# Attention beside a state-space convolution: x relaid out by VectorE instead of GpSimd, and zero matmuls sized to what a group lacks

## The chip, the cores and the metric

The kernel runs on one core of a Trainium2 chip. The metric is the device time of one execution in microseconds; a time is the median of several runs. The engines that matter are TensorE (PE in the profile; its weight loads are PEld), ScalarE (ACT), VectorE (DVE), GpSimd (POOL) and SyncE (SP, which here issues nearly all DMAs). Each engine works through its own list of instructions in order; semaphores make one engine wait for another.

## The reference

Two branches work on the same x (2048 rows of 512, bf16) and are mixed by a gate. In short:

```python
g = sigmoid((x * gate_w).sum(-1, keepdims=True))
# A: attention, 32 heads of 16, no mask
q, k, v = split(x @ wqkv)
a = softmax(q @ k.T * 16 ** -0.5) @ v     # per head, 2048 x 2048 scores
a = a @ wo
# B: a state-space layer: a causal convolution along the rows, 512 channels, 128 states each
P = exp(dt * A * l)                       # l = 0..2047, complex
K = einsum(C, P, dt * B).real             # 512 x 2048
b = causal_conv(x, K) + x * Dskip
return g * a + (1 - g) * b
```

## The kernel before

**The two branches.** Attention is cut into 32 blocks b (a quarter of the queries, a pair of key/value column groups, one of two head parities) and each block into 16 steps kt of 128 keys. One step has four score tiles of 128 x 512, one per row group of the array. ScalarE takes three score tiles at a time: a *group* g is one `ex(g)`, an exponential of 128x1536 from a PSUM tile SC (three banks) to the ring ET; there are 683 groups. `qk(g)` makes the three score tiles of a group with three matmuls of 32 rows each, and two SC tiles alternate, so the scores of group g + 1 can be made while ScalarE works on group g, and those of g + 2 only when g is done. `pv(q)` multiplies four tiles of ET by V with four matmuls of 32 columns each, which add up in the bank OA over the 16 steps of a block. At a block's end `norm_a` transposes OA to SBUF (VectorE, L704), `norm_b` divides by the sums, and OA is free for the next block.

The state-space branch is done in chunks of 64 rows. VectorE builds the powers of the transition (params, base, table: L718 and others). Then, for each of four quarters qr of the channels: the x rows of the chunks are multiplied into states on TensorE (`sstage`, evicted from PSUM bank MB at L1006), a scan over 32 chunks runs on VectorE (L1026 to L1042), and the output is formed on TensorE (`ystage`, evicted at L1114). This work needs x in another layout: with 64 positions of a chunk on partitions and chunk and channel along the free axis. `rows` loads it from a DRAM copy of x with two DMAs (L1129, issued by SP), into XS for the states and into XR for the output. In this layout an element's channel is the inner index and the chunk the outer one (32 x 64), while the matmuls want 64 channels by 32 chunks. GpSimd turns it round: two multiplications by a half mask hm per quarter, from XS to XZ (L1141), and one copy per quarter from XR to X2 (L1151). XZ is the moving operand of the state matmuls, X2 that of the local part of the output.

The projections, the gate, the convolution's kernel and the final projection use the bank MB as well, one user at a time (a lock in the scheduler), and VectorE evicts it.

**What sets the order.** The order on every engine is laid down when the program is made. `record` walks through the groups. For each it emits `ex(g)` and `qk(g + 1)`, then calls `sch.fill(t, .5, zeros, quiet())`, where t is the planned end of the exponential on ScalarE. The scheduler holds threads (Python generators: `pvs`, `norms`, `qms`, `projs`, `ystage`, `scan`, `ublks`, `ulocals` and so on). Each yields an engine, a planned cost and a priority ahead of a few instructions, and may ask for marks of others (AFTER) or for MB (LOCK). `fill` issues the thread that can start earliest, as long as it can start before t, and for TensorE work of lower rank ends before t + 0.5. Planned costs stand in the code; a DMA is planned with its issue cost, a latency, and LATE (2.0) more before its reader may start. AFTER marks order the plan alone; on the chip only data dependences wait.

**Zero matmuls.** `wm` is a tile of zeros. `zeros()` multiplies it (128 x 128 by 128 x 512) into OA, so it adds nothing to an open block. It is issued in two places: in `fill`, ahead of a background TensorE piece of lower rank, and at a group's end while TensorE's planned time is before t. It needs an open block (`sch.now`, set by `sch.open` after each `pv` and set to None after the last step of a block). At most two are issued per group. `p.act` adds up the activity of what was issued: a matmul's columns times the share of the array that it fills (128 for one score or one PV matmul, 512 for a zero matmul). After each group `lack[0]` gains FILL (1300) minus `p.act`, held between 0 and 512; `zeros()` issues when `lack[0]` is at least 256. Besides, the groups run in cycles of 17. In 12 of them state and output matmuls ("low" pieces) may be issued; in the other 5, the quiet ones, low pieces wait and zero matmuls are issued whatever `lack` says.

All matmuls are recorded in the helper at L562, so the profile's groups are told apart by their tiles.

Of the kernel before, what the change touches and what calls it, by code (L numbers as in the profile page):

```python
# [20 lines left out]
CB = D // NBLK  # L21
HALF_PI = math.pi / 2
NDSEM = 56
FILL = 1300
NS = 15
SGH = 144
NSG = 2
LATE = 2.0
CYCLE, LOWS = 17, 12
VW = 152  # L30


# [205 lines left out]
class Sched:  # L238


    def __init__(self, prog):
        self.p = prog
        self.thr = []
        self.flag = set()
        self.lock = {}
        self.now = None
        self.n = 0

    def add(self, gen, prio):
# [12 lines left out]
        else:  # L262
            self.flag.add(name)

    def open(self, b):
        if self.p.cap is not None:
            self.p.cap.append(lambda: self.open(b))
        else:
            self.now = b

    def unlock(self, name):
        if self.p.cap is not None:
# [4 lines left out]
    def pull(self, t):  # L277
        t.conds, t.seg = [], None
        y = t.nxt
        if y is None:  # L280
            y = next(t.gen, None)
        while y is not None and y[0] in ("AFTER", "LOCK"):
            t.conds.append(y)
            y = next(t.gen, None)
        if y is None:
            assert not t.conds
            return
        t.eng, t.cost = y[0], y[1]
        t.up = y[2] if len(y) > 2 else t.prio
        t.low = len(y) > 3  # L290
        assert self.p.cap is None
        self.p.cap = []
        t.nxt = next(t.gen, None)
        t.seg, self.p.cap = self.p.cap, None
        if t.nxt is None:
            t.gen = iter(())
# [29 lines left out]
        if t.seg is None:  # L326
            self.thr.remove(t)

    def fill(self, until, slack, zeros, quiet=False):
        while True:  # L330
            best = None
            for t in self.thr:
                if t.low and quiet:
                    continue
                e = self.est(t)
                if e is None or e > until or t.eng == "PE" and t.up > 0 and e + t.cost > until + slack:
                    continue
                now = self.p.tm[t.eng]
                k = (max(e, now + .3) if e > now + .02 else now, t.up, t.n)
                if best is None or k < best[0]:  # L340
                    best = (k, t)
            if best is None:
                break
            if best[1].eng == "PE" and best[1].up > 0 and zeros():
                continue
            self.issue(best[1])
        while self.p.tm["PE"] < until and zeros():
            pass

    def force(self, name):  # L350
# [12 lines left out]
class Thread:  # L363

    def __init__(self, gen, prio, n):
        self.gen, self.prio, self.n = gen, prio, n
        self.nxt = None
        self.conds, self.seg, self.eng, self.cost, self.up, self.low = [], None, None, 0, prio, False


def declare(nc, es):
# [76 lines left out]
    for k in range(4):  # L448
        sb(f"X2{k}", 32 * 64)
        sb(f"XZ{k}", 2 * 32 * 64)  # L450
        sb(f"XS{k}", 32 * 64)
        sb(f"XR{k}", 32 * 64)

    sb("Py", 3 * 2 * 16 * T)
# [92 lines left out]
def record(nc, p, B, ins):  # L547
# [533 lines left out]
    def ystage():  # L1081
        yield ("AFTER", "gp")

        def unit(u):
            blk, hf = divmod(u, 2)
            qr, bl = divmod(blk, 4)
            sg, r = SG[qr % NSG], u % 3
            yield ("AFTER", f"scan{qr}")
            yield ("AFTER", f"ul{qr}")
            yield ("AFTER", f"yl{u}")  # L1090
            yield ("LOCK", "MB")
            ky = [(MB, 0, ('y', u))]
            for k in range(8):
                if k % 4 == 0:
                    yield ("PE", .28, 2, True)
                kk = 8 * hf + k
                mm(lambda k=k: MB(32 * k, [[1, 32]]), lambda k=k: Tt(r * 1024 + 128 * k, [[1, 128]]),
                   lambda kk=kk: X2[qr](32 * (16 * bl + kk), [[1, 32]]),
                   [(X2[qr], 0)] + [(Tt, (r, par, k // 4), u) for par in range(2)] + [(Tt, "z")], ky, k == 0, False, c=.1 if k % 4 == 0 else .06, a=32)
            for k in range(8):  # L1100
                if k % 2 == 0:
                    yield ("PE", .48, 2, True)
                kk = 8 * hf + k
                for ri in range(2):
                    for par in range(2):
                        i = 2 * k + par
                        mm(lambda k=k, par=par: MB(32 * k, [[1, 32]], 64 * par, 64),
                           lambda ri=ri, i=i: Py(r * YN + ri * 16 * T + i * T, [[1, T]]),
                           lambda ri=ri, kk=kk, par=par: sg(ri * SGH + CB * bl + 2 * kk + par, [[2 * SGH, 32]]),
                           [(sg, (bl, b_), (qr, 'G')) for b_ in range(4)] + [(sg, "z"), (Py, r, u)], ky, False, ri == 1,  # L1110
                           pos=(0, 64 * par), c=.1 if k % 2 == ri + par == 0 else .056, a=16)
            sch.mark(f"yu{u}")
            yield ("DVE", .4, -1)
            op("DVE", lambda v: v.tensor_tensor(Yl(16 * blk + 8 * hf, [[256, 32], [1, 8]]), MB(0, [[1, 32], [32, 8]]),  # L1114
                                                B["g1"](0, [[1, 32], [0, 8]]), ALU.mult), ky + key("g1"), [(Yl, u)], c=.38)
            sch.unlock("MB")
            if u % 8 == 7:
                sch.mark(f"yq{qr}")

        for u in range(2 * NBLK):  # L1120
            yield from unit(u)

    hm = B["hm"]
    poolq = [(hm, "q")]

    def rows(b, qr):
        for par in range(2):
            yield ("SP", 1.9)
            dma("SP", lambda e, par=par: e.dma_start(b(0, [[64, 32], [1, 64]], 64 * par, 64),  # L1129
                                                     B["xrd"].dram(64 * qr + 256 * par, [[32 * D, 64], [D, 32], [1, 64]])),  # L1130
                [(B["xrd"], 0)], [(b, par)], c=1.9, lat=5)

    def ublocks(qr):
        XS = B[f"XS{qr}"]
        yield ("AFTER", f"yu{8 * qr - 12}" if qr >= 2 else f"S{4 * qr - 2}" if qr else "base3")
        yield from rows(XS, qr)
        if qr:
            yield ("AFTER", f"S{4 * qr - 1}")
        for h in range(2):
            yield ("POOL", 3.5)  # L1140
            op("POOL", lambda g, h=h: g.tensor_scalar(XZ[qr](32 * h, [[64, 64], [1, 32]]), XS(0, [[1, 64], [64, 32]]), hm(h, [[1, 1]]), None, ALU.mult),  # L1141
               [(XS, 0), (XS, 1), (hm, 0)], [(XZ[qr], h)] + poolq, c=3.5)
        sch.mark(f"ub{qr}")

    def ulocal(qr):
        XR = B[f"XR{qr}"]
        yield ("AFTER", f"S{4 * qr + 3}")
        yield ("AFTER", "K15")
        yield from rows(XR, qr)
        yield ("POOL", 3.5)  # L1150
        op("POOL", lambda g: g.tensor_copy(X2[qr](0, [[32, 64], [1, 32]]), XR(0, [[1, 64], [64, 32]])),  # L1151
           [(XR, 0), (XR, 1)], [(X2[qr], 0)] + poolq, c=3.5)
        sch.mark(f"ul{qr}")

    def ublks():
# [105 lines left out]
    def pvs():  # L1261
        for q in range(NQ - 1):
            b, kt = divmod(q, 16)
            if kt == 0 and b >= 1:
                yield ("AFTER", f"n{b - 1}")
            if b < 8 and b % 2 == 0 and kt % 4 == 0:
                yield ("AFTER", f"V{b // 2}.{kt // 4}")
            yield ("PE", QUAD)
            pv(q)
            sch.mark(f"pv{q}")  # L1270
            sch.open(b if kt < 15 else None)

    def norms():
        for b in range(31):
            yield ("AFTER", f"pv{16 * b + 15}")
            yield ("DVE", .75, -2)
            norm_a(b)
            sch.mark(f"n{b}")
            yield ("DVE", .65, 1)
            norm_b(b)  # L1280
            if b % 2 == 1:
                yield ("DVE", .7, 1)
                norm_c(b)
# [62 lines left out]
    def quiet():  # L1346
        return p.q % CYCLE >= LOWS

    def zeros():
        b = sch.now  # L1350
        if lack[0] < 256 and not quiet() or lack[1] == 2 or b is None:
            return False
        mm(lambda: OA(0, [[1, 512]]), lambda: wm(0, [[1, 128]]), lambda: wm(0, [[1, 512]]), [(wm, 0)], [(OA, 0, b)], False, False)
        lack[0] -= 512
        lack[1] += 1
        p.act -= 512
        return True

    for g in range(NG):
# [8 lines left out]
            need(g + 1)  # L1368
            qk(g + 1)
        t = p.tm["ACT"]  # L1370
        sch.fill(t, .5, zeros, quiet())
        lack[0] = max(min(lack[0] + FILL - p.act, 512), 0)
        p.act = lack[1] = 0
    while sch.thr:
        p.q += 1
        sch.fill(1e9, 1e9, lambda: False)
        assert p.q < NG + 50, [(t.conds, t.eng, t.prio) for t in sch.thr]

    p.q += 1
# [46 lines left out]
```

## Time and profile before

| | |
|---|---|
| median of three runs | 1041.11 us (1034.61, 1041.11, 1050.18) |
| the profiled execution | 1036.27 us, its span 1034.5 us |
| granted TensorE clock, mean over the span | 0.81 |
| instructions in the trace | 17282 |
| HBM read, written | 30.02 MB, 25.17 MB |
| share of 16 DMA engines, queue q1 | 29.8% |
| x rows XS, XR: DMAs of 256 KB | 8 and 8; 5.1 and 5.3 us from issue to landing (median) |

The page gives, after the busy time of each engine, the span in 40 slices of 25.9 us. A digit is the busy share in tenths; PEclk is the share of TensorE's full clock that was granted. Of a group of instructions it gives line, engine and operation, the tiles written and read, shape and number, then busy time and mean duration (ns), then the engine's idle time just before them and what ended most of it. In a timeline each row has start, duration, engine, line and operation; the idle time before it and its releaser stand in square brackets. A table of stretches gives, for each, its length, the busy time and number of instructions per engine (PE, PEld, DVE, ACT, POOL), the granted clock, the DMA share and GB/s.

The mean duration of a matmul holds its passage through the array; matmuls behind each other start closer than that.

### The profile page before, as it was taken

Reading aid. Unit: us, or ns where it says so; the run is one execution under the profiler, and the core shown is the slowest. Engines: PE = TensorE matmul, PEld = TensorE weight load, DVE = VectorE, ACT = ScalarE, POOL = GpSimd, SP = SyncE. Lnnn points to the kernel's source line nnn. Section 1 sums busy time; section 2 is a strip of 40 time slices with the busy share of each in tenths; the row PEclk is TensorE's granted clock in tenths of the full one; section 3 lists DMA queues with packets and bytes.
Section 4 is the critical chain, followed back from the end, with each engine's and each line's share of the span. In section 5 each row is a group of like instructions: output and inputs, shape, how many; then the busy total and the mean of one; then the engine's idle time right before and its main releaser. Section 6 shows DMA issues by size and latency. Waiting matters only on the chain.

```text
span 1034.5 us, 17282 instructions
## 1 busy us (share of the span) xinstructions
PE 868.8 (84%) x7323; PEld 280.1 (27%) x7323; DVE 663.5 (64%) x1329; ACT 936.9 (91%) x693; POOL 89.8 (9%) x28
## 2 busy tenths in 40 slices
PE   7888858898968799878858988499889998987896
PEld 3233222222322222112312223132233333332211
DVE  5899989977796888898992259951299411131202
ACT  6999959999969999988959999499999999899995
POOL 4000230000050000120320010500100000000000
PEclk9999969877858977766958689666898799699866
DMA  8200100028655556261413464034212221010000
GB/s 178 82 2 1 22 1 1 1 93 199 152 90 151 143 143 152 115 128 52 98 51 67 67 123 98 26 78 59 44 52 78 77 78 52 11 37 16 1 1 21
DMA packets 171469, 73.35 MB, mean 71 GB/s; under 512 B 150272, under 2 KB 159104, under 8 KB 169344
## 3 DMA queue, kind: packets, MB, share of 16 engines
q1 hardware_dynamic: 169088, 71.07, 29.8%
q10 hardware_dynamic: 2304, 1.18, 0.6%
q8 instruction: 57, 0.93, 0.4%
q14 instruction: 20, 0.16, 0.1%
HBM read 30.02 MB, written 25.17 MB: 53 GB/s over the span
## 4 chain that ended last, share of the span: by engine, by line
ACT 52%; PE 28%; DVE 17%; DMA 1%; issue 1%; ACTq 0%; DVEq 0%
ACT ET L690 52%; PE OA L562 14%; PE SC L562 9%; PE MB L562 5%; DVE G L1039 3%; DVE s L1032 2%; DVE s L1035 2%; DVE SG L1042 2%; DVE s L1029 2%; DVE tt L718 1%; DVE ft L718 1%; DVE Qm L666 1%; DVE SG L1006 1%; DMA Wq<-in_A_wqkv_dram 1%; DVE ON L709 1%
## 5 line engine op out<-in xcount | busy, mean ns | idle before, releaser
L690 ACT ACTIVATE ET<-SC 128x1536 bf16<-128x1536 f32 (+1 forms) x683 | 929.8, 1609 | 81.2 <-PE SC L562 79.6
L562 PE MATMUL SC<-Qm,KT 32*128 32x512 bf16 x2048 | 310.8, 449 | 89.1 <-ACT ET L690 81.4
L562 PE MATMUL OA<-ET,VE 128*32 128x512 bf16 x2048 | 239.3, 458 | 30.5 <-DVE OT L704 29.6
L562 PE MATMUL OA<-wm 128*128 128x512 bf16 x587 | 233.2, 454 | 1.2 <-DVE wm L615 1.2
L562 PEld LDWEIGHTS SC<-Qm,KT 32*128 32x128 bf16 x2048 | 68.0, 93 | 288.0 <-ACT ET L690 219.0
L1006 DVE TENSOR_TENSOR SG<-MB,sgn 128x496 bf16<-128x496 f32 x64 | 42.9, 670 | 94.7 <-PE MB L562 94.6
L562 PEld LDWEIGHTS OA<-ET,VE 128*32 128x32 bf16 x2048 | 54.2, 96 | 179.0 <-issue 140.9
L1141 POOL TENSOR_SCALAR XZ<-XS,hm 128x2048 bf16<-128x2048 bf16 x8 | 59.8, 7481 | 282.9 <-DMA XS<-gm_xrd 170.1
L562 PEld LDWEIGHTS OA<-wm 128*128 128x128 bf16 x587 | 43.4, 100 | 120.0 <-issue 118.8
L718 DVE TENSOR_TENSOR tt<-B,D 128x1024 bf16<-128x1024 bf16 x96 | 67.1, 734 | 0.5
L704 DVE STREAM_TRANSPOSE OT<-OA 128x512 f32<-128x512 f32 x32 | 22.8, 713 | 60.8 <-PE OA L562 60.7
L1039 DVE TENSOR_TENSOR G<-s,s 128x256 f32<-128x256 f32 x120 | 59.2, 493 | 3.4
L1114 DVE TENSOR_TENSOR Yl<-MB,g 128x256 bf16<-128x256 f32 x32 | 13.4, 419 | 73.3 <-PE MB L562 73.1
L1032 DVE TENSOR_TENSOR s<-G,MU 128x256 f32<-128x256 f32 x120 | 58.8, 490 | 0.0
L1035 DVE TENSOR_TENSOR s<-s,SG 128x256 f32<-128x256 f32 x120 | 55.4, 461 | 0.0
L562 PE MATMUL MB<-XZ,Qt 128*128 128x64 bf16 x512 | 40.9, 216 | 12.9 <-DVE SG L1006 12.2
L1029 DVE TENSOR_TENSOR s<-G,MU 128x256 f32<-128x256 f32 x120 | 50.1, 418 | 0.1
L562 PE MATMUL MB<-SG,Py 128*64 128x32 bf16 x1024 | 47.3, 233 | 2.2 <-DVE SG L1042 2.2
L562 PEld LDWEIGHTS MB<-XZ,Qt 128*128 128x128 bf16 x512 | 29.7, 110 | 44.8 <-issue 27.3
L666 DVE TENSOR_SCALAR Qm<-Q,msk 128x512 bf16<-128x512 bf16 x31 | 17.4, 562 | 35.0 <-PE SC L562 35.0
L1042 DVE CAST SG<-G 128x256 bf16<-128x256 f32 x120 | 37.6, 313 | 3.5
L718 DVE TENSOR_TENSOR ft<-FP,L 128x1024 f32<-128x1024 f32 (+1 forms) x32 | 39.1, 1244 | 0.3
(128 smaller groups left out, 513.5 us busy)
## 6 DMA issues: line engine op xcount, KB each, us to landing
gm_ptd<-PT SPq DMA_DIRECT2D x16, 1024.0 KB, 6.1
Py<-gm_ptd SPq DMA_DIRECT2D x32, 512.0 KB, 4.1
gm_kpd<-Kst SPq DMA_DIRECT2D x16, 256.0 KB, 2.5
Tt<-gm_kpd SPq DMA_DIRECT2D x128, 32.0 KB, 3.3
gm_xrd<-in_A_x_dram SPq DMA_DIRECT2D x1, 2048.0 KB, 12.0
XS<-gm_xrd SPq DMA_DIRECT2D x8, 256.0 KB, 5.1
XR<-gm_xrd SPq DMA_DIRECT2D x8, 256.0 KB, 5.3
out_dram<-fo SPq DMA_DIRECT2D x28, 64.0 KB, 2.1
```

Source lines behind the costliest of these rows:

```text
L562: op("PE", lambda t: t.matmul(out(), lhsT(), rhs(), start=start, stop=stop, skip_group_check=True, **kw), R, W, c=c, lat=.15, a=a)
L666: op("DVE", lambda v: v.tensor_scalar(Qm(512 * (b % 2), [[1, 512]]), B[f"Q{qc}"](512 * pi, [[1, 512]]), msk(w, [[1, 1]]), None, ALU.mult), ...
L690: op("ACT", lambda a: a.activation(ET(512 * e, [[1, 512 * n]]), sc(0, [[1, 512 * n]]), AF.Exp, scale=DH ** -0.5), [(sc, i, g) for i in ran ...
L704: op("DVE", lambda v: v.transpose(OT(0, [[1, 512]]), OA(0, [[1, 512]])), [(OA, 0, b)], [(OT, 0, b)], c=.72)
L718: op(eng, lambda v: v.tensor_tensor(o(), a(), b_(), f), R, W, c=c)
L1006: op("DVE", lambda v, bank=bank: v.tensor_tensor(sg(2 * SGH + CB * bl + 8 * bank, [[2 * SGH, 31], [SGH, 2], [1, 8]]), MB(0, [[1, 31], [256 ...
L1029: op(e, lambda v: v.tensor_tensor(s2(0, [[128, 2], [1, 128]]), G(0, [[128, 2], [1, 128]]), MU(d0, [[0, 2], [1, 128]]), ALU.mult), key("G", ...
L1032: op(e, lambda v: v.tensor_tensor(s3(0, [[128, 2], [1, 128]]), G(128, [[-128, 2], [1, 128]]), MU(D + d0, [[D, 2], [1, 128]]), ALU.mult), k ...
L1035: op(e, lambda v, so=so: v.tensor_tensor(s2(0, [[128, 2], [1, 128]]), s2(0, [[128, 2], [1, 128]]), sg(so, [[SGH, 2], [1, 128]]), ALU.add), ...
L1039: op(e, lambda v: v.tensor_tensor(G(0, [[1, 256]]), s2(0, [[1, 256]]), s3(0, [[1, 256]]), ALU.add), [(s2, 0), (s3, 0)], [(G, 0)], c=.38)
L1042: op(e, lambda v, so=so: v.tensor_copy(sg(so, [[SGH, 2], [1, 128]]), G(0, [[128, 2], [1, 128]])), key("G"), ks if c < NCH - 2 else [(sg, ( ...
L1141: op("POOL", lambda g, h=h: g.tensor_scalar(XZ[qr](32 * h, [[64, 64], [1, 32]]), XS(0, [[1, 64], [64, 32]]), hm(h, [[1, 1]]), None, ALU.mult),
```

## The change

**Relayout.** GpSimd's two multiplications (L1141) and its copy (L1151) go. `rows` now takes an output tile too: after its two DMAs VectorE copies the tile round in two halves of 32 channels (128x1024 each). For the states the copy goes into a new buffer XP, four of 4 KB per partition, and VectorE multiplies XP by hm into XZ (128x2048, twice per quarter); for the output the copy goes straight into X2, of which both halves are then read dependences of the output matmuls.

**Zero matmuls.** A new function `want` says how many columns a group still lacks: 512 in a quiet group, otherwise FILL minus `p.act` plus the carried lack, plus EDGE (384) while kt 13 or 14 is the last step issued; never more than 1024 per group. `zeros` issues one matmul of that many columns (up to 512, in steps of 32, none under 96). The zero matmuls no longer go ahead of background; they come at the group's end, with no bound by TensorE's planned time, and ahead of a block's last PV (the one step yielded with a fifth value, `t.end`). When a low piece is weighed, the price of what is lacking (0.45 ns a column) is added to it. After `norm_a` the freed bank counts as open (`sch.open("z", 0)`), as soon as the plan has the transposition done before the end of the exponential; zero matmuls there begin a new accumulation, which the next block's first PV overwrites. FILL becomes 1400, the carried lack is at most 384, and a cycle is 20 groups with 15 low ones.

```diff
-FILL = 1300
+FILL = 1400
-CYCLE, LOWS = 17, 12
+CYCLE, LOWS = 20, 15
+EDGE = 384
...
-                if e is None or e > until or t.eng == "PE" and t.up > 0 and e + t.cost > until + slack:
+                if e is None or e > until or t.eng == "PE" and t.up > 0 and e + t.cost + (lack() * .00045 if t.low else 0) > until + slack:
...
-            if best[1].eng == "PE" and best[1].up > 0 and zeros():
-                continue
+            while best[1].end and zeros():
+                pass
             self.issue(best[1])
-        while self.p.tm["PE"] < until and zeros():
+        while zeros():
             pass
...
-    def rows(b, qr):
+    def rows(b, o, qr):
         for par in range(2):
             yield ("SP", 1.9)
             dma("SP", lambda e, par=par: e.dma_start(b(0, [[64, 32], [1, 64]], 64 * par, 64),
...
+        for k in range(2):
+            yield ("DVE", 1.15)
+            op("DVE", lambda v, k=k: v.tensor_copy(o(1024 * k, [[32, 32], [1, 32]]), b(32 * k, [[1, 32], [64, 32]])),
+               [(b, 0), (b, 1)], [(o, k)], c=1.15)
...
         for h in range(2):
-            yield ("POOL", 3.5)
-            op("POOL", lambda g, h=h: g.tensor_scalar(XZ[qr](32 * h, [[64, 64], [1, 32]]), XS(0, [[1, 64], [64, 32]]), hm(h, [[1, 1]]), None, ALU.mult),
-               [(XS, 0), (XS, 1), (hm, 0)], [(XZ[qr], h)] + poolq, c=3.5)
+            yield ("DVE", .75)
+            op("DVE", lambda v, h=h: v.tensor_scalar(XZ[qr](32 * h, [[64, 64], [1, 32]]), XP(0, [[32, 64], [1, 32]]), hm(h, [[1, 1]]), None, ALU.mult),
+               [(XP, 0), (XP, 1), (hm, 0)], [(XZ[qr], h)], c=.75)
...
     def ulocal(qr):
...
-        yield from rows(XR, qr)
-        yield ("POOL", 3.5)
-        op("POOL", lambda g: g.tensor_copy(X2[qr](0, [[32, 64], [1, 32]]), XR(0, [[1, 64], [64, 32]])),
-           [(XR, 0), (XR, 1)], [(X2[qr], 0)] + poolq, c=3.5)
+        yield from rows(B[f"XR{qr}"], X2[qr], qr)
...
-            yield ("PE", QUAD)
+            yield ("PE", QUAD, 0, 0, 0) if kt == 15 else ("PE", QUAD)
             pv(q)
             sch.mark(f"pv{q}")
-            sch.open(b if kt < 15 else None)
+            sch.open(b if kt < 15 else None, kt)
...
             norm_a(b)
             sch.mark(f"n{b}")
+            sch.open("z", 0)
...
+    def want():
+        n = 512 if quiet() else FILL - p.act + lack[0] + (EDGE if sch.kt in (13, 14) else 0)
+        if sch.now is None or sch.now == "z" and p.ready((0, ("PE", 0, (), [(OA, 0)]))) > p.tm["ACT"]:
+            return 0
+        return max(0, min(n, 1024 - lack[1]))
+
     def zeros():
-        b = sch.now
-        if lack[0] < 256 and not quiet() or lack[1] == 2 or b is None:
+        b, n = sch.now, min(512, want() // 32 * 32)
+        if n < 96:
             return False
-        mm(lambda: OA(0, [[1, 512]]), lambda: wm(0, [[1, 128]]), lambda: wm(0, [[1, 512]]), [(wm, 0)], [(OA, 0, b)], False, False)
-        lack[0] -= 512
-        lack[1] += 1
-        p.act -= 512
+        mm(lambda: OA(0, [[1, n]]), lambda: wm(0, [[1, 128]]), lambda: wm(0, [[1, n]]), [(wm, 0)], [(OA, 0, b)], b == "z", False, c=.015 + n * .00042, a=n)
+        lack[1] += n
         return True
...
-        sch.fill(t, .5, zeros, quiet())
-        lack[0] = max(min(lack[0] + FILL - p.act, 512), 0)
+        sch.fill(t, .5, zeros, want, quiet())
+        lack[0] = max(min(lack[0] + FILL - p.act, 384), 0)
         p.act = lack[1] = 0
```

## The prediction

> **What bounds the kernel now.** I read the page's busy shares first, then the slices, ScalarE's waits, and the timelines around the longest waits.
>
> ```profile
> PE 868.8 (84%) x7323; PEld 280.1 (27%) x7323; DVE 663.5 (64%) x1329; ACT 936.9 (91%) x693; POOL 89.8 (9%) x28
> ...
> ACT  6999959999969999988959999499999999899995
> ...
> PEclk9999969877858977766958689666898799699866
> ...
> L690 ACT ACTIVATE ET<-SC 128x1536 bf16<-128x1536 f32 (+1 forms) x683 | 929.8, 1609 | 81.2 <-PE SC L562 79.6
> ...
> L1141 POOL TENSOR_SCALAR XZ<-XS,hm 128x2048 bf16<-128x2048 bf16 x8 | 59.8, 7481 | 282.9 <-DMA XS<-gm_xrd 170.1
> ```
>
> ScalarE is the bound: 683 exponentials (groups of three score tiles) fill 91% of the span. In the chain the stretch from 18.07 us holds 78 of them in 104.76 us; less one duration (1.45) that is 77 steps of 1.342 us. What can be won is the idle time between them, and all of it waits for score matmuls:
>
> ```profile
> ACT ET L690 <- PE SC L562: 79.6, 78, 12.9
> ```
>
> ScalarE's timeline splits the 79.6 us in two. Six waits are over 2 us: 9.61, 2.86, 5.50, 3.52, 10.99 and 12.85, 45.3 us in all. The other 72 are at most 1.51 us, 34.3 us in all. The two kinds have different causes.
>
> The first kind, by the timelines of GpSimd, VectorE, TensorE and ScalarE around 134 us:
>
> ```profile
> 123.98 15.64 POOL L1141 TENSOR_SCALAR XZ<-XS,hm 128x2048 bf16<-128x2048 bf16 x2 [112.45 <-issue]
> ```
> ```profile
> 125.01 5.18 DVE L718 TENSOR_TENSOR nwi<-u,u 128x512 bf16<-128x512 f32 x1
> 130.12 1.53 DVE L866 TENSOR_SCALAR MU<-MU 128x512 f32<-128x512 f32 x1
> 131.57 7.41 DVE L718 TENSOR_TENSOR ft<-FP,L 128x1024 f32<-128x1024 f32 x2
> ...
> 141.61 0.69 DVE L660 CAST VE<-MB 128x512 bf16<-128x512 f32 x1
> ```
> ```profile
> 142.36 1.03 PE L562 MATMUL MB<-Wv,xT 128*128 128x128 bf16 x8 [9.69 <-DVE VE L660]
> ```
> ```profile
> 144.53 1.45 ACT L690 ACTIVATE ET<-SC 128x1536 bf16<-128x1536 f32 x1 [9.61 <-PE SC L562]
> ```
>
> While GpSimd runs a 7.4 us relayout, one VectorE operation on SBUF takes 5 to 7 us instead of 0.4 to 1.2. VectorE works in order, so an eviction of bank MB comes late; TensorE works in order too, so the next scores stand behind the matmul that wants MB. All six long waits lie in or just behind such a relayout (starts 124.0 and 131.5, 292.2 and 299.4, 444.8, 509.1 and 516.7, 646.6 and 653.8).
>
> The second kind, by the busy times of two neighbouring stretches and TensorE's timeline in the first:
>
> ```profile
> 235.38:238.79 3.41, 2.14 (x19) 0.59 (x16) 3.27 (x6) 3.41 (x4) 0.00 (x0) 1.00 1.06 171
> 238.79:242.21 3.42, 2.86 (x18) 0.61 (x18) 3.32 (x6) 3.42 (x4) 0.00 (x0) 0.51 1.04 188
> ```
> ```profile
> 236.22 0.39 PE L562 MATMUL SC<-Qm,KT 32*128 32x512 bf16 x3 [0.79 <-ACT ET L690]
> 236.54 0.40 PE L562 MATMUL OA<-ET,VE 128*32 128x512 bf16 x4
> 236.87 0.39 PE L562 MATMUL OA<-wm 128*128 128x512 bf16 x1
> 237.56 0.39 PE L562 MATMUL SC<-Qm,KT 32*128 32x512 bf16 x3 [0.30 <-ACT ET L690]
> ```
>
> The clock column (third from the end) falls from 1.00 to 0.51. The granted clock changes only on a grid of 3.41 us and is either full or half, so I added up each cell of that grid: a matmul's columns times the share of the array it fills (a score matmul, 32 rows, counts 128; four PV matmuls 512; a zero matmul 512). After the 28 full-speed cells that were followed by half speed the sums are 2958 or less; of the 158 followed by full speed, 154 are above 2958. A half-speed cell ends in full speed from 3018 up and stays at half up to 3047. So some 2950 holds the clock and some 3030 brings it back. At half speed a group with two zero matmuls outlasts its exponential:
>
> ```profile
> 592.86 1.03 PE L562 MATMUL OA<-wm 128*128 128x512 bf16 x2
> 593.83 0.61 PE L562 MATMUL SC<-Qm,KT 32*128 32x512 bf16 x3
> 594.37 0.62 PE L562 MATMUL OA<-ET,VE 128*32 128x512 bf16 x4
> 594.91 1.03 PE L562 MATMUL OA<-wm 128*128 128x512 bf16 x2
> ```
>
> Scores to scores (593.83 to 595.88) is 2.05 us, 0.71 over the 1.342. The clock is at half for 395 us of the span, in 28 stretches, and almost all 72 short waits lie there. At full clock exponentials follow each other without loss.
>
> **The change part by part.** Its sum stands against the profiled execution: 1036.27 us, a span of 1034.5 and 1.8 around it. That is 4.8 under the median shown (1041.1).
>
> *Relayout off GpSimd.* Twelve GpSimd operations go (8 of 7.4 us, 4 of 3.7). GpSimd keeps four small memsets of SG (0.34 to 0.55 us) and one of Tt (2.66), which stood in its queue behind them. The six long waits go. Idle is counted from an end to a start, and an exponential that follows without idle starts 0.11 before the last one ends (1.45 long, 1.342 apart), so each wait costs 0.11 more than its idle: 45.3 + 6 x 0.11 = 46.0 us.
>
> In place come 24 VectorE operations: 16 copies of 1024 elements that gather at a stride of 64, and 8 multiplications of 2048 by the half mask. No row has such a copy. Below, the 128x1024 bf16 copy of L923 is 0.42; above, the 128x2048 cast of L899, twice the elements, is 1.22. I take 1.0, nearer the long end since the gather is the less regular one, and the same for the multiplications: 24 us (10 to 29). VectorE idles 371 us now and loses about 50 us of stretched operations, so on average it is covered. Where it is not: two copies back to back put up to 2.4 us ahead of a transposition or an eviction, eight times, against about 0.9 us by which scores are ready ahead of need; (2.4 - 0.9) x 8 = 12 us. I take 1.
>
> The Trainium skill, "VectorE: DVE Perf Modes", section "What auto-detection actually checks", would let a one-source copy inside SBUF use two ports whatever its inner stride; by its per-operation terms an estimate is 0.7 us a copy, which would make the 24 us some 17. No run here shows it.
>
> *A new wait on VectorE.* The copies wait in VectorE's order for x rows by DMA; GpSimd did so before, with nobody behind. The 16 DMAs of SP stay, two per relayout, in the same order. They take 5.1 and 5.3 us to land (6.7 at most); the scheduler's prices (1.9 for the issue, 5 to land, LATE of 2) place a copy no sooner than 8.9 us after the issue. Behind a waiting copy stand the transposition of OA, Qm and the evictions of MB. I take nothing; at worst 2 us at each of eight places, 16.
>
> *Zero matmuls.* Counted in the order of TensorE's instructions: 861 behind the first group in place of 578, with 397,568 columns in place of 295,936. The 101,632 more are 198 times 512, at 0.215 (the step from one to two such matmuls in the timeline, 0.39 to 0.60) 43 us of TensorE. Cover: at full clock scores take 0.32 (236.22 to 236.54), PV 0.33, two zero matmuls about 0.44, so 1.09 of 1.342. Where background stands too, the new price held back in front of low background and the slack of 0.5 let TensorE fall behind by some tenths; I take 1 us, at most 5.
>
> What they bring, in the same count: over 2.55 consecutive groups (3.41 / 1.34), 87 of 681 positions of the old order are below 2950, the lowest 2170. In the new order none is; the lowest is 3158. FILL at 1400, the extra 384 at steps kt 13 and 14, the fills ahead of the last PV and in the freed bank make a block's end as full as its middle; 5 of 20 groups are kept quiet in place of 5 of 17, and this does not reopen a hole. So the clock should fall only where TensorE is held up. The 72 short waits go: 34.3 + 72 x 0.11 = 42.2 us. I leave 3 us for a few half-speed stretches (one costs 42.2 / 28 = 1.5).
>
> The skill speaks against this part: "TensorE: Matmul & The Clock Gate", section "HAM oscillation", gives as the rule 'no PE-idle gaps >~3.4µs'. The longest idle in the cell above is 0.79 us, and the clock fell. By the rule the zero matmuls bring nothing and the sum is 990; by the count it is what follows.
>
> *Sum.* From above: 1036.3 - 46.0 - 42.2 + 1 + 1 + 3 = 953. From below: first exponential at 14.2, 682 steps of 1.342 = 915.2, a last one of 1.1, 11.4 behind it (last PV, normalisation, output), 1.8 around: 943.7, and with the same 5 us 949. The 4 us between are the steps inside merged rows, which at full clock are often nearer 1.33 (682 x 0.012 = 8 less). I take **946 us**, 0.908 of the median, with 936 (steps of 1.33 and nothing left) to 960 as its own range.
>
> **The rivals.**
> *The clock isn't held.* If zero-filled groups lose their effect, only the long waits go, and the half-speed stretches that began at them: 1036 - 46 - 0 to 11 = 979 to 990, say 985. For it: 4 of 158 cells stayed up below 2958, so the count isn't sharp. Against it: 3158 is 7% above.
> *New waits in the queues.* Zero matmuls in the freed bank wait for OA's transposition, with scores behind them. If each of 31 block ends costs one transposition (0.7), 22 us: 968; with late x rows up to 16 more.
> *Slower: TensorE bound at half clock.* The heavier groups (mean 582 zero columns, before 433) take longer at half speed: scores 512 columns, PV 384, zeros 582, background about 220 at 1.2 columns per ns, and some 0.35 for switches and small matmuls, 1.77 us, 0.43 over the step. Saturated, a cell holds about 3000 to 3300, near the 3030 that wakes the clock. It is slower than 1041 once half speed covers (1041 - 946) / (683 x 0.43) = 32% of the span, and by over 2% from 39%; now it covers 38%. Against it: with nothing below 3158 the clock must first fall.
>
> **How the numbers follow.** The forecast has 0.80, the clock 0.10, new waits 0.05, TensorE at half speed 0.05. Two per cent is about what a measurement here can tell from no change. Only the last case reaches it: within 2% 0.02, slower 0.03, so faster 0.95. The range 935 to 972 holds the forecast and the queue waits and leaves the clock case and the slow one out.
>
> **What would show it.** Right: no L1141 on POOL; no VectorE operation of 5 us; ScalarE waits over 2 us gone and the wait for scores below 10 us; clock above 0.95. Wrong: copies of over 1.3 us, or their wait for XS rows; waits of the first OA zero matmul for the transposition with ScalarE idle behind; half-speed cells whose sum is above 2958.

## The result and the profile after

The changed kernel takes 945.8 us (median of four runs, 945.2 to 946.6), the kernel before 1043.7 in the same comparison: a ratio of 0.909, with a 95% interval of 0.903 to 0.915. The forecast was 946. The profiled execution took 945.2 us, its span 943.4.

The page of the changed kernel, in the lines that answer to those of before: busy shares, ScalarE and the granted clock in 40 slices, the chain by engine, and the exponentials.

```profile
PE 790.8 (84%) x7493; PEld 271.1 (29%) x7606; DVE 634.4 (67%) x1353; ACT 924.8 (98%) x693; POOL 14.6 (2%) x16
...
ACT  6999999999999999999999999999999999999995
...
PEclk9999999999999999999999999999999999999998
...
ACT 96%; PE 1%; DMA 1%; DVE 1%; issue 0%; ACTq 0%; DVEq 0%
...
L693 ACT ACTIVATE ET<-SC 128x1536 bf16<-128x1536 f32 (+1 forms) x683 | 917.6, 2021 | 2.7 <-PE SC L565 2.7
```

ScalarE is busy in every slice between the first and the last, and the chain is now 96% ScalarE (52% before). The wait for scores, 79.6 us in 78 waits before, is one wait of 2.7 us, the first exponential's. The clock is at full from 12.1 us to 937.1 us. The half-speed stretches that are left lie before the first and behind the last exponential.

The first exponential's wait stood among the 78 before too, as ScalarE's timeline of the kernel before shows:

```profile
14.21 1.45 ACT L690 ACTIVATE ET<-SC 128x1536 bf16<-128x1536 f32 x1 [2.96 <-PE SC L562]
```

The stretches of the changed kernel, between the first exponential and the last (length, then busy time of PE, PEld, DVE, ACT, POOL, then clock, DMA share and GB/s):

```profile
14.00:500.00 486.00, 405.96 (x3625) 133.30 (x3679) 435.03 (x847) 486.00 (x365) 3.33 (x3) 1.00 0.38 91
500.00:932.00 432.00, 373.81 (x3810) 133.11 (x3863) 185.45 (x465) 431.92 (x322) 0.67 (x2) 1.00 0.27 59
```

ScalarE is busy for 917.9 of 918.0 us. There is nothing left to win by feeding it: what remains is 13.6 us ahead of the first exponential, 682 steps of 1.345 us on average, and 11.3 us behind the last.

The relayout's operations on VectorE, from the view of the tile XP (duration in ns, least, median and greatest):

```profile
L1136 DVE COPY XP<-XS x8: 1003/1038/1060, 199.8 to 610.0; 128x1024 bf16<-128x1024 bf16 x8
L1147 DVE TENSOR_SCALAR XZ<-XP,hm x8: 737/750/758, 203.6 to 612.0; 128x2048 bf16<-128x2048 bf16 x8
```

With the eight copies into X2 (1.04 us) that is 16 x 1.04 + 8 x 0.75 = 22.6 us of VectorE. No VectorE operation on SBUF is stretched to 5 us any more.

### The profile page after: what moved, and what is told of

It reads as the page before. It is cut to its first block, busy times and chain, and to the rows that moved or that the text cites. A ratio compares the mean times of both kernels' runs of the same rounds, so it can differ in the third digit from the quotient of the medians.

```text
span 943.4 us, 17746 instructions
## 1 busy us (share of the span) xinstructions
PE 790.8 (84%) x7493; PEld 271.1 (29%) x7606; DVE 634.4 (67%) x1353; ACT 924.8 (98%) x693; POOL 14.6 (2%) x16
## 4 chain that ended last, share of the span: by engine, by line
ACT 96%; PE 1%; DMA 1%; DVE 1%; issue 0%; ACTq 0%; DVEq 0%
ACT ET L693 96%; DMA Wq<-in_A_wqkv_dram 1%; PE OA L565 1%; PE SC L565 0%; PE MB L565 0%; DVE fo L1208 0%; ACTq L569 0%; DVE OT L707 0%; DVE OnT L717 0%; DVE KT L654 0%; ACT e L781 0%; ACT ea L779 0%; DVE ON L712 0%; DVE Rz L711 0%; ACT ge L1185 0%
## 5 line engine op out<-in xcount | busy, mean ns | idle before, releaser
L693 ACT ACTIVATE ET<-SC 128x1536 bf16<-128x1536 f32 (+1 forms) x683 | 917.6, 2021 | 2.7 <-PE SC L565 2.7
L565 PE MATMUL SC<-Qm,KT 32*128 32x512 bf16 x2048 | 267.1, 385 | 113.8 <-ACT ET L693 90.9
L565 PE MATMUL OA<-wm 128*128 128x512 bf16 (+5 forms) x769 | 240.4, 363 | 14.7 <-issue 11.3
L565 PE MATMUL OA<-ET,VE 128*32 128x512 bf16 x2048 | 204.9, 391 | 3.5 <-DVE OT L707 3.0
L565 PEld LDWEIGHTS OA<-wm 128*128 128x128 bf16 x870 | 60.5, 97 | 84.5 <-issue 68.4
L1032 DVE TENSOR_TENSOR s<-G,MU 128x256 f32<-128x256 f32 x120 | 50.1, 418 | 0.1
L1035 DVE TENSOR_TENSOR s<-G,MU 128x256 f32<-128x256 f32 x120 | 50.0, 417 | 0.0
L565 PEld LDWEIGHTS MB<-SG,Py 128*64 128x64 bf16 x1024 | 30.5, 116 | 28.9 <-issue 28.8
L721 DVE TENSOR_TENSOR PT<-tt,tt 128x1024 bf16<-128x1024 bf16 x48 | 32.8, 684 | 0.5
L565 PE MATMUL MB<-XZ,Qt 128*128 128x64 bf16 x512 | 29.5, 195 | 0.0
L1208 DVE SCALAR_TENSOR_TENSOR fo<-MB,g,Yl 128x256 bf16<-128x256 f32 x24 | 11.6, 484 | 25.4 <-PE MB L565 24.9
```

Source lines behind the costliest of these rows:

```text
L565: op("PE", lambda t: t.matmul(out(), lhsT(), rhs(), start=start, stop=stop, skip_group_check=True, **kw), R, W, c=c, lat=.15, a=a)
L693: op("ACT", lambda a: a.activation(ET(512 * e, [[1, 512 * n]]), sc(0, [[1, 512 * n]]), AF.Exp, scale=DH ** -0.5), [(sc, i, g) for i in ran ...
L721: op(eng, lambda v: v.tensor_tensor(o(), a(), b_(), f), R, W, c=c)
L1032: op(e, lambda v: v.tensor_tensor(s2(0, [[128, 2], [1, 128]]), G(0, [[128, 2], [1, 128]]), MU(d0, [[0, 2], [1, 128]]), ALU.mult), key("G", ...
L1035: op(e, lambda v: v.tensor_tensor(s3(0, [[128, 2], [1, 128]]), G(128, [[-128, 2], [1, 128]]), MU(D + d0, [[D, 2], [1, 128]]), ALU.mult), k ...
L1208: op("DVE", lambda v, c2=c2, c=c: v.scalar_tensor_tensor(o(off + 256 * c2, [[1, 256]]), b(bo + 256 * c2, [[1, 256]]), B["g"](c, [[1, 1]]), ...
```

## The experiments

The theory in test: two causes that are largely separate. One is GpSimd's relayout, which stretches VectorE's operations and so, through bank MB, TensorE's scores. The other is a clock that falls when a cell of 3.41 us holds too few columns times filled share of the array. The rivals: the clock falls only because TensorE is held up; the long waits came from the plan or from waiting for XZ, not from contention; TensorE's busy time counts, not the area; and a smaller or larger FILL would do.

### Each part alone

The relayout alone (the old rule for zero matmuls; the cycle of 20/15 is the one number taken along, and by it the old rule issues 535 of them behind the first group, where it issued 578):

```diff
+        sb(f"XP{k}", 32 * 64)
...
-    def rows(b, qr):
+    def rows(b, o, qr):
...
+        for k in range(2):
+            yield ("DVE", 1.15)
...
-CYCLE, LOWS = 17, 12
+CYCLE, LOWS = 20, 15
```

> The kernel before with the relayout on VectorE and its old zero matmuls (only the cycle of quiet groups is 20/15, so that the buffers fit). Two-cause theory: the six long ScalarE waits go (46 us), the half-speed stretches stay; by the count of the instruction order 110 of 681 positions are below 2950 (87 before), so 980 to 1000 us, clock 0.80 to 0.88. Rival, the half speed follows from the stalls (the clock falls only when TensorE is held up): both go, 946 to 955 us, clock above 0.97.

Measured: 987.9 us, a ratio of 0.945 (0.939 to 0.951) to the kernel before on the same chip. ScalarE's wait for scores and the clock:

```profile
ACT ET L691 <- PE SC L563: 32.0, 75, 3.7
```
```profile
PEclk7999999869776889676695667679868997897967
```

The longest of the 75 waits, 3.7 us, is the first exponential's. No wait is over 2 us once the exponentials run, yet 74 short ones remain (28.3 us) and the clock's mean is 0.81 as before. The stalls didn't cause the half speed: that rival falls.

The zero matmuls alone (the changed kernel with L1141 and L1151 of before):

```diff
-        sb(f"XP{k}", 32 * 64)
...
-        yield from rows(XS, XP, qr)
+        yield from rows(XS, qr)
...
-            yield ("DVE", .75)
+            yield ("POOL", 3.5)
...
```

> The changed kernel with the relayout back on GpSimd. Two-cause theory: the long waits of 46 us stay, and the clock falls only behind them (six times, some 2 us each): 985 to 1010 us, clock 0.92 to 0.97. Rival, the long waits are a matter of the plan around the old zero matmuls: 946 to 960 us.

Measured: 1016.5 us, 0.973 (0.969 to 0.978).

```profile
ACT ET L692 <- PE SC L564: 65.5, 50, 12.5
```
The long waits are back, six of them: 9.20, 5.15, 6.73, 12.53, 2.49 and 10.77, 46.9 us. Of the other 44, one is the first exponential's (2.6 us); 43 short ones make 16.0 us, more than I had allowed (the measured time is 6 us above the range). All but one lie in the half-speed stretches behind the long waits, which last 13.7 to 37.5 us. TensorE's timeline shows one of them in the middle:

```profile
527.53 0.62 PE L564 MATMUL OA<-ET,VE 128*32 128x512 bf16 x4
528.08 0.42 PE L564 MATMUL MB<-SG,Py 128*64 128x32 bf16 x8
528.43 0.48 PE L564 MATMUL OA<-wm 128*128 128x352 bf16 x1
528.84 0.61 PE L564 MATMUL SC<-Qm,KT 32*128 32x512 bf16 x3
```

TensorE has no idle here, and once it has no idle the cells of this stretch hold 2563 to 3030: saturated and still below what wakes the clock. It woke after two groups with two whole zero matmuls each, by a cell of 3152.

The parts save 56 us and 27 us; together they save 98. By the profiled executions (1036.3 before) it is 47, 19 and 91. So 15 to 25 us come only with both. The rows fit this: zero matmuls can't hold the clock through a stall, when TensorE does nothing, and the short waits behind the six stalls stay. Whether they also make the half speed behind a stall longer is open: its stretches last 13.7 to 37.5 us here and 17.1 to 30.7 before.

### Is it contention, or the wait for XZ?

GpSimd work that nobody reads, beside the changed kernel (the first two lines only let the search for buffer places go on longer):

```diff
-    for k in range(4000):
+    for k in range(40000):
...
+        for h in range(2):
+            yield ("POOL", 3.5)
+            op("POOL", lambda g, h=h: g.tensor_scalar(XP(0, [[32, 64], [1, 32]]), XS(0, [[1, 64], [64, 32]]), hm(h, [[1, 1]]), None, ALU.mult),
+               [(XS, 0), (XS, 1), (hm, 0)], [(XP, 0), (XP, 1)], c=3.5)
         sch.mark(f"ub{qr}")
```

> The changed kernel, and beside it eight GpSimd multiplications of XS by hm (two per quarter, 7 us each, as before) into XP after its last reader; their result is read by nobody. Theory, GpSimd's operation stretches VectorE's by itself: VectorE operations of 5 us come back in eight places, 975 to 1005 us. Rival, the stalls came from waiting for XZ or from the plan: 946 us, VectorE's durations unchanged.

Measured: 993.3 us in one run. GpSimd's and VectorE's timelines around one pair:

```profile
501.48 14.80 POOL L1151 TENSOR_SCALAR XP<-XS,hm 128x2048 bf16<-128x2048 bf16 x2 [83.40 <-DVE XZ L1147]
```
```profile
501.20 0.42 DVE L1038 TENSOR_TENSOR s<-s,SG 128x256 f32<-128x256 f32 x1
501.65 5.54 DVE L1042 TENSOR_TENSOR G<-s,s 128x256 f32<-128x256 f32 x1
507.22 1.56 DVE L1045 CAST SG<-G 128x256 bf16<-128x256 f32 x1
508.70 0.41 DVE L1032 TENSOR_TENSOR s<-G,MU 128x256 f32<-128x256 f32 x1
509.03 0.41 DVE L1035 TENSOR_TENSOR s<-G,MU 128x256 f32<-128x256 f32 x1
509.37 5.47 DVE L1038 TENSOR_TENSOR s<-s,SG 128x256 f32<-128x256 f32 x1
```

The stretched operation is 5.5 us instead of 0.42, once per GpSimd operation (4.5 to 5.8 us in all eight), and nothing waits for the result of GpSimd. Four waits of ScalarE over 2 us follow: 8.37, 7.19, 10.40 and 10.24, one per pair. It is contention. The Trainium skill, "GPSIMD Engine Reference", section "Key points", says that GpSimd shares its SBUF interfaces with VectorE and lists two-input operations among those that contend. The rows agree, and add that one operation pays for nearly all of it.

The same work in 64 pieces of 256 elements (the diff is against the run just told):

```diff
-            op("POOL", lambda g, h=h: g.tensor_scalar(XP(0, [[32, 64], [1, 32]]), XS(0, [[1, 64], [64, 32]]), hm(h, [[1, 1]]), None, ALU.mult),
+            for i in range(8):
+                op("POOL", lambda g, h=h, i=i: g.tensor_scalar(XP(256 * i, [[32, 8], [1, 32]]), XS(8 * i, [[1, 8], [64, 32]]), hm(h, [[1, 1]]), None, ALU.mult),
...
```

> The idle GpSimd work of the earlier run in eight pieces each (64 operations of 256 elements instead of 8 of 2048). If an operation of GpSimd keeps VectorE from its memory for as long as it lasts, and VectorE gets its turn between pieces, VectorE's stretched operations are under 1.5 us and 946 to 960 us follow. If the contention is by amount of work, the stretches add up as before: 980 to 1000 us.

Measured: 955.2 us in one run. The view of the tile XP for GpSimd's pieces, and VectorE's timeline behind the first of them:

```profile
L1152 POOL TENSOR_SCALAR XP<-XS,hm x64: 1146/1327/2004, 206.2 to 642.1; 128x256 bf16<-128x256 bf16 x64
```
```profile
490.44 0.81 DVE L1042 TENSOR_TENSOR G<-s,s 128x256 f32<-128x256 f32 x1
491.28 0.29 DVE L1045 CAST SG<-G 128x256 bf16<-128x256 f32 x1
491.49 0.42 DVE L1032 TENSOR_TENSOR s<-G,MU 128x256 f32<-128x256 f32 x1
491.83 0.42 DVE L1035 TENSOR_TENSOR s<-G,MU 128x256 f32<-128x256 f32 x1
492.16 0.87 DVE L1038 TENSOR_TENSOR s<-s,SG 128x256 f32<-128x256 f32 x1
```

GpSimd is busy longer than with whole operations (64 x 1.33 = 85 us against 8 x 7.36 = 59, by the medians), and VectorE loses 0.4 us here and there instead of 5 at once. TensorE has the same matmuls in the same order in both runs, so the plan is no part of the difference. So the harm is set by how long one GpSimd operation lasts, not by how much GpSimd does. The 9 us that remain over the changed kernel are waits of ScalarE (7.5 us more) and three half-speed stretches.

### What the clock counts

The changed kernel in the same order, each zero matmul on 32 rows of the array:

```diff
-        mm(lambda: OA(0, [[1, n]]), lambda: wm(0, [[1, 128]]), lambda: wm(0, [[1, n]]), [(wm, 0)], [(OA, 0, b)], b == "z", False, c=.015 + n * .00042, a=n)
+        mm(lambda: OA(0, [[1, n]]), lambda: wm(0, [[1, 128]], 0, 32), lambda: wm(0, [[1, n]], 0, 32), [(wm, 0)], [(OA, 0, b)], b == "z", False, pos=(0, 0), c=.015 + n * .00042, a=n)
```

> The changed kernel in the same order, but each zero matmul uses 32 rows of the array instead of 128 (same columns, same time at a given clock). Area theory, a cell needs columns times filled share of some 2950: a zero matmul counts a quarter, 419 of 681 positions fall below, the clock is at half for most of the span and seldom wakes: 1080 to 1250 us, clock 0.5 to 0.7. Rival, what counts is that TensorE is busy: 946 us, clock 0.99.

Measured: 1069.6 us in one run, mean clock 0.62.

```profile
PE 1019.6 (95%) x7606; PEld 306.0 (29%) x7606; DVE 636.2 (60%) x1353; ACT 958.4 (90%) x693; POOL 14.6 (1%) x16
...
PEclk7999998556665556555555555555555555559955
```

TensorE is 95% busy, more than in any other run, and the clock is at half for 809 us. Counted by area, the nine falls from full speed come after cells of 2950 or less, and between the exponentials no cell that kept full speed holds under 3040. Counted as if a zero matmul of 32 rows filled the array, the eight falls between the exponentials come after 3200 to 4710 though cells of 3650 kept full speed, and cells of up to 4340 stay at half speed though one of 3130 woke: no threshold fits. So the rival falls. The time is 10 us below my range: a 0.25 us loss per half-speed step where I had worked with 0.43.

Then the dose (1200, and in a second kernel 1100):

```diff
-FILL = 1400
+FILL = 1200
```

> FILL 1200 in place of 1400. Threshold theory: in the instruction order one position of 681 is below 2950 (the plain run of groups sums to 3060), so the clock holds: 945 to 951 us, clock above 0.97, with 69,000 fewer zero columns. Rival, the wide margin above the threshold is needed because groups shift against the cells: 955 to 985 us.

> FILL 1100. Threshold theory: 177 positions below 2950, the plain run of groups at 2805, so the clock falls in most groups that are not quiet: 965 to 1010 us, clock 0.65 to 0.85, though TensorE is never idle for 1.5 us. Rival, a rule by idle gaps: 946 us, clock 0.99.

Measured: 972.0 us (969 and 975) at 1200, 991.5 us (990.9 and 992.2) at 1100. For 1200 my expectation was wrong: the clock is at half for 240 us, in 18 stretches between the exponentials and at both ends. Two neighbouring stretches of that run show one fall, behind a cell of 2999, and TensorE's timeline what stood in the first:

```profile
298.30:301.70 3.40, 2.08 (x26) 0.90 (x27) 3.27 (x6) 3.40 (x4) 0.00 (x0) 1.00 0.22 38
301.70:305.10 3.40, 3.40 (x19) 0.67 (x16) 3.40 (x7) 3.40 (x3) 0.00 (x0) 0.51 1.01 112
```
```profile
298.58 0.39 PE L565 MATMUL SC<-Qm,KT 32*128 32x512 bf16 x3 [0.35 <-ACT ET L693]
298.96 0.29 PE L565 MATMUL MB<-XZ,Qt 128*128 128x64 bf16 x4
299.93 0.39 PE L565 MATMUL SC<-Qm,KT 32*128 32x512 bf16 x3 [0.68 <-ACT ET L693]
300.25 0.40 PE L565 MATMUL OA<-ET,VE 128*32 128x512 bf16 x4
```

(Some records of zero matmuls are missing in this trace; the sums put them back from the weight loads and the order of the program.) The falls come after cells of 2656 to 2999, as the threshold has it. What failed is my count: 2.55 groups with their mean filling come to 3060, but a cell is filled in lumps. Its 3.41 us can begin behind one group's work and end ahead of another's zero matmuls, and then it holds two groups and the scores of a third, 2 x 1200 + 384 = 2784.

By that smallest cell FILL 1300 gives 2984 and 1400 gives 3184:

```diff
-FILL = 1400
+FILL = 1300
```

> FILL 1300 in the changed kernel. Mended theory, after FILL 1200 fell short: the smallest cell holds two groups and the next one's scores, 2 x 1300 + 384 = 2984, just above 2950 (1400: 3184, 1200: 2784), so the clock nearly holds: 945 to 953 us, clock above 0.96. Rival, the time falls evenly with FILL between 972 (1200) and 946 (1400): 957 to 961 us, clock about 0.93.

Measured: 950.9 us (949.2 to 953.4), mean clock 0.96. This is the mended theory's, not the straight line's. Its falls come after cells of 2934 to 3009, so the threshold is nearer 3010 than my 2950; four cells of 2976 to 3008 kept full speed all the same. In the changed kernel the smallest full-speed cell between the exponentials holds about 3080 (3050 in its second trace).

### The block's end, and more zeros

Without the fill in the freed bank, without EDGE, and without the fill ahead of the last PV:

```diff
-EDGE = 384
+EDGE = 0
...
-            while best[1].end and zeros():
-                pass
...
-            sch.open("z", 0)
```

> The changed kernel without its three measures at a block's end (no fill in the freed bank, EDGE 0, none ahead of the last PV); the sizing and the filling behind the background stay. Theory: 14 positions below 2950, all at block ends, each a half-speed stretch of 1.5 to 3 us: 960 to 985 us, clock 0.88 to 0.96. Rival, the sizing alone is enough: 946 us.

Measured: 952.4 us (948.6 and 956.3), clock 0.976 in the profiled run. My range was too high: 14 low positions became five half-speed stretches between the exponentials. The rival (946) is nearer, though not met. The three measures at the block's end are worth some 3 to 10 us; the sizing and the place behind the background, which no run separates, are worth the rest of the zero matmuls' gain.

More zeros:

```diff
-FILL = 1400
+FILL = 1800
```

> FILL 1800: 184,000 zero columns more, up to the cap of 1024 in most groups. Theory: at full clock the cover of 1.34 us per group still holds: 945 to 952 us, clock 0.99. Rival, TensorE becomes the bound (lags of some tenths a group): over 960 us.

Measured: 1004.3 us. Neither theory: the exponentials run as in the changed kernel and end at 931.7 us (932.1 there), but the span is 1002.4.

```profile
500.00:931.00 431.00, 394.16 (x3667) 126.07 (x3729) 172.44 (x435) 431.00 (x322) 0.68 (x2) 1.00 0.27 56
931.00:1002.40 71.40, 38.74 (x442) 25.98 (x439) 23.21 (x49) 0.75 (x1) 0.00 (x0) 0.52 0.20 49
```

TensorE didn't slow ScalarE. The output matmuls came late, as the view of the tile Yl shows for this run and then for the changed kernel (its evictions, with first and last start):

```profile
L1117 DVE TENSOR_TENSOR Yl<-MB,g x32: 386/425/426, 447.5 to 943.6; 128x256 bf16<-128x256 f32 x32
```
```profile
L1117 DVE TENSOR_TENSOR Yl<-MB,g x32: 403/424/425, 436.1 to 833.7; 128x256 bf16<-128x256 f32 x32
```

The last eviction starts at 943.6 us, against 833.7 in the changed kernel, and the final projection comes after the last exponential, at half clock. By the code, what pushes them back is the larger price of what is lacking, added when a low piece is weighed, or the planned time of the zero matmuls themselves; no run tells these two apart. The cost of too many zeros is the background's place, and it shows only at the end.

### The start

From the profile after, the one half-speed cell ahead of the first exponential looked like 1 to 2 us to be had:

```diff
-    for k in range(9):
+    for k in range(26):
```

> The changed kernel with 26 warming zero matmuls ahead of the first projection instead of 9, enough to reach the landing of Wq at about 8.8 us. Theory: the half-speed cell at 8.7 us goes, the first projections and scores take about half of 3.5 us, 944 to 945 us, 1 to 2 us under the changed kernel on the same chip. Rival: the start waits for DMA alone, no difference, or the longer zero row delays the projection: 946 to 948 us.

> The changed kernel itself, for the others of this call: 945 to 947 us.

Measured side by side: 946.9 us (945.5 to 948.4) with 26, 945.9 us (945.2 to 947.5) for the changed kernel. TensorE's timeline of the first, and then of the second:

```profile
1.19 7.12 PE L565 MATMUL OA<-wm 128*128 128x512 bf16 x26 [1.19 <-DVE wm L618]
8.14 0.83 PE L565 MATMUL SC<-idb,x0n 128*128 128x128 bf16 x12
...
13.09 0.60 PE L565 MATMUL SC<-Qm,KT 32*128 32x512 bf16 x6 [1.33 <-DVE KT L654]
```
```profile
4.84 0.84 PE L565 MATMUL SC<-idb,x0n 128*128 128x128 bf16 x12
...
9.08 1.89 PE L565 MATMUL OA<-xT,Wq 128*128 128x512 bf16 x4 [3.18 <-DMA Wq<-in_A_wqkv_dram]
...
13.46 1.03 PE L565 MATMUL SC<-Qm,KT 32*128 32x512 bf16 x6 [0.79 <-DVE KT L654]
```

The clock did stay up, but the zeros took the place in which the transposes of x had run. Those slipped from 4.84 to 8.14 us, and their evictions with them. No gain, as the rival had it (946 to 948); the changed kernel stands as the best of these.

## Why the prediction was right

The time, 946 against 945.8, is closer than its working deserves, since small errors cancelled.

- *The six long waits, 46.0 us.* Right, and the mechanism is shown by the idle GpSimd work. Over the 1.345 us of the changed kernel these six steps had lost 47.5 us. The relayout alone saved 56 us by the medians and 47 between the profiled executions (1036.3 and 989.4); its time, 987.9, lies in the 979 to 990 that the rival of a clock that isn't held had for it.
- *The 24 VectorE operations, 24 us, of which 1 on the path.* The copy was taken at 1.0 us and is 1.04; the multiplication was taken at 1.0 and is 0.75; nothing of it is on the path. The estimate from the Trainium skill, "VectorE: DVE Perf Modes", section "What auto-detection actually checks", was 0.7 us a copy; the rows have 1.04, so here the gather at a stride of 64 doesn't get all that the two ports would give.
- *The wait for x rows, nothing.* Right: VectorE has no idle that ends on XS or XR.
- *The 72 short waits, 42.2 us less 3.* The mechanism is right: by area and with a threshold on the 3.41 us grid. The reading of the waits was off by one. Over 2 us there are seven, not six; the seventh is the first exponential's, which nothing in the change was to remove; it is 2.96 us before and 2.66 after. The other 71 are 31.3 us, 39.1 by the same working. The 3 us held back for half-speed stretches weren't needed either, since no fall between the exponentials remained, so the two slips cancel by luck: 39.2 was taken, and over 1.345 us those 71 steps had lost 39.3. Another 4.0 us came from steps with too little idle to be listed as a wait. The rule of the Trainium skill, "TensorE: Matmul & The Clock Gate", section "HAM oscillation", of idle gaps beyond 3.4 us, would have made the zero matmuls worthless (990 for the changed kernel). The changed kernel has 945.8, the relayout with the old zero matmuls 987.9, and at FILL 1100 the clock falls though TensorE is never idle for over 0.78 us between the exponentials.
- *The count over 2.55 groups.* Its result (none below 2950) was right, its form wrong. FILL 1200 passed it at all but one position and fell 18 times. Two groups and the next scores are the nearer measure, though still a rough one: they give 2784, 2984 and 3184 at FILL 1200, 1300 and 1400, and the smallest full-speed cells between the exponentials hold 2656, 2934 and some 3080.
- *The floor.* The sum from above was 953 and lacked 8 us: the waits were worth 5.6 more than taken, and the 2 us of costs on VectorE and TensorE can't be seen. I came down to 946 for another reason, that the steps at full clock are often nearer 1.33, for 8 us. They average 1.345 in the changed kernel (the most frequent is 1.33), so that gain doesn't exist, and that it stood in for the other is luck. The sum from below without any costs, 943.7, was the better one: 1.5 under the profiled execution.
- *The slow rival*, zero matmuls that keep TensorE saturated at half clock, is real: the zero matmuls alone show a stretch of 37.5 us, with cells of 2563 to 3030 where TensorE has no idle. It didn't decide because with the relayout gone no cell between the exponentials lets the clock fall first. It may be a part of why the second part is worth 27 us alone and 42 beside the first; no run measures that part.

## What to carry to other kernels

Split an engine's idle time by length before explaining it: the six long waits and the short ones had different causes, and each half of the change answered one. Where the clock must be held, look at the emptiest stretch on its grid, not at the mean, and add only what that stretch lacks: at FILL 1200 it fell 18 times, and at 1800 the background was pushed past the end. An engine off the critical path can hold up the one on it by the length of a single operation; where work must stay on GpSimd here, short pieces cost 9 us where long ones cost 47.

## What the runs showed of the hardware

- Near one threshold the clock changes in both directions. The sum is columns times filled share of the array per cell of 3.41 us, the columns spread from 0.06 us behind a matmul's recorded start. In the eight traces that lack hardly any matmul record (before, the second trace of the changed kernel, the relayout alone, the zero matmuls alone, both runs with idle GpSimd work, the narrow zero matmuls, FILL 1300), between the exponentials, all 84 falls come after cells of some 3014 or less, all 87 returns after some 3008 or more, and none of 446 cells that stayed at half is above 3048. It isn't sharp for the falls: of 1643 cells that kept full speed 11 hold under 3010, down to 2752, and why they kept it is open. With 512 columns in 0.215 us a full-speed cell could hold some 8100, an estimate.
- What counts is the filled area: TensorE at 95% busy with 32-row zero matmuls stood at half speed for 809 of 1068 us.
- A GpSimd operation of 7.4 us stretched one VectorE operation from 0.42 to 5.5 us, and let a few others through before it ended (two of 0.41 in the rows above); pieces of 1.33 us stretched them by 0.4.
